# Regrouping the products of exponentials and v in an attention stage into two pairs

## The chip, the cores and the metric

The kernel runs on one core of a Trainium2 chip. Its engines work side by side, each through its own queue in order: TensorE (PE in the profile, its weight loads PEld), VectorE (DVE), ScalarE (ACT), GpSimd (POOL) and SyncE (SP), which issues most of the transfers. TensorE writes its results into PSUM banks, from which ACT and DVE take them. The metric is the device time of one execution in microseconds; the time of a version is the median of its runs.

## The reference

A transformer block over one sequence of 2048 tokens with 576 channels: adaptive layer norm, causal attention in four segments of 512 tokens with 32 heads of 18 channels and a memory of the earlier segments, then a second layer norm and a gated feed-forward network of 4608 channels. The change touches the attention inside a segment:

```python
for s in range(N):
    qs, ks, vs = q[:, :, s], k[:, :, s], v[:, :, s]
    logits = jnp.einsum("bhqd,bhkd->bhqk", qs, ks) * scale + mask
    p = _softmax(logits, axis=-1)
    a_dot = jnp.einsum("bhqk,bhkd->bhqd", p, vs)
    ...
    a_mem = num / den
    o = g * a_mem + (1.0 - g) * a_dot
```

## The kernel before

The kernel has three stages. The first projects q, k and v and writes them to DRAM. The second is the attention, with the output projection and the second layer norm woven into it. The third is the feed-forward network, which takes two thirds of the time and is bound by TensorE. Only the second stage is touched by the change.

The second stage goes over 32 units. Unit u = 8s + q is segment s and a group q of four heads. The order of all instructions is written out by hand (`manual_schedule`, L1160, and the loop at L1168): each turn of the loop has eleven steps, and each step emits three things.

- One step of `p2_step` (L565) for unit u: the logits, transposed, in a PSUM bank with tag s2 (two banks, L576), their exponential on ACT into the tile P0, P1, P2 or P3 (L579), and, at the end of each P, the causal mask on POOL (L583). Steps 0 to 3 fill P0 (keys 0 to 127, 512 queries), 4 to 7 fill P1 (384 queries), 8 and 9 P2 (256), 10 P3 (128).
- One step of `p1_step` (L164) for unit u + 2: the logits a second time, in a bank with tag s1 (two banks, L174), and the row maxima on DVE (L179). Its steps are equally wide, 512 for steps 0 to 3, 384 for 4 to 7, then 256 and 128. The maxima of a unit are transposed (`mt_a`, L193), copied and sent to DRAM (`mt_b`, L197 and L198) and loaded back (`load_m`, L161) as two more rows of q, so that the logits of `p2_step` come out with the maximum subtracted. A unit's first logits wait for that load.
- A list of events, from the table PAT (L54). It has four rows of eleven strings: row 0 for even units with q below 4, row 1 for odd ones, row 2 for even units with q of 4 and more, row 3 for odd ones. A step's events are emitted in the order of its string, behind the products of that step.

The events that matter here, as `event` (L807) resolves them:

- V0, V1 (of unit u) and V2, V3 (of unit u - 1): `av_step` (L587), the products of exponentials and v. Each is four products in fp32, one for each head, with 32 columns of the array each; they accumulate over V0 to V3 into one PSUM bank, av. V0 has 512 columns of queries, V1 384, V2 256, V3 128. A product in fp32 is two loads and two passes, so that a group shows as eight rows.
- E: the copy of av to SBUF on ACT (L608); c: four transposes of it (L617); d: division and weighting on DVE (L625 to L634).
- m and n: `mt_a` and `mt_b` with the load, for unit u + 1.
- M0 to M3 and X: a quarter each of the 14 products of a half row of the output projection (L694), and its addition on DVE (L699); R, S, T and Z, z prepare its operands by transposes (L666, L654) and copies.
- g and h: three activations on ACT (L743 to L745) and an addition on POOL for phi(q), in units with q below 5 and s below 3. D, G, A0, A1, B0, B1, C: the memory's part for q of 4 and more (products at L765, copies at L774).
- l, p, x: the second layer norm of a finished block, with an activation of 576 columns on ACT at x (L726), in odd units. Q, q, Y, P, f: small preparations.

The loop that emits them:

```python
            for k in range(11):
                next(ga, None)
                next(gb, None)
                for ev in PAT[q // 4 * 2 + u % 2][k].split():
                    event(ev, u)
```

Of the kernel before, what the change touches and what calls it, by code (L numbers as in the profile page):

```python
# [15 lines left out]
P = 128  # L16
S = 2048
D = 576
# [32 lines left out]
NE = 2  # L51
E1 = 3
E2 = 2
PAT = (["", "V2", "V3 E m D", "M0", "n M1 Q G", "c", "M2 d", "V0 g", "h A0 q M3 R S X", "T Y Z B0", "A1 P V1 z B1 f C"],  # L54
# [3 lines left out]
LNA = 1  # L58
S1B, S2B, XB, WB = 2, 2, 2, 1

# [6 lines left out]
def block(ctx: ExitStack, tc: tile.TileContext, x, wqk, wv, wo, beta, wgu, wd, c, w_mod, out):  # L67
# [1092 lines left out]
    with tc.manual_schedule():  # L1160
# [7 lines left out]
        for u in range(NU + 1):  # L1168
# [176 lines left out]
```

## Time and profile before

| | us |
|---|---|
| median of 3 runs | 1945.69 |
| lowest and highest run | 1944.17, 1946.47 |
| span of the profiled execution | 1946.8 |
| attention stage in it (first to last product of the 33 turns) | 260 to 618 |

The page gives no time of the profiled execution beside its span. In the rows of the timeline stand the start and the length in microseconds, the engine, the line, the operation, what it writes and reads, the size, and in brackets how long the engine was idle before it and what released it. A product's length includes its way through the array, so that successive products overlap; what one takes of TensorE's time is read from start to start. In the tables by stage, the columns are the stretch, its length, the busy time of PE, PEld, DVE, ACT and POOL with the number of instructions, the clock granted to TensorE (1 is full), the busy share of the DMA engines and the GB/s moved.

### The profile page before, as it was taken

How to read it: one execution, taken by the hardware profiler on the slowest of the kernel's cores; microseconds unless marked ns; L12 is line 12 of the kernel's file. 1: busy time of each engine (PE TensorE's matmuls, PEld its weight loads, DVE VectorE, ACT ScalarE, POOL GpSimd, SP SyncE). 2: the span in 40 equal slices, each digit the busy share in tenths (PEclk: the TensorE clock that was granted, in tenths of full speed). 3: DMA queues.
4: the chain of work that ended last, by engine and by line, in shares of the span. 5: the costliest groups of instructions: out<-in, count | busy, mean ns of one | idle time of the engine just before them, and what ended most of it. 6: DMA issues, size and time to landing. Idle time of an engine off the chain costs nothing.

```text
span 1946.8 us, 31901 instructions
## 1 busy us (share of the span) xinstructions
PE 1901.2 (98%) x11119; PEld 1593.1 (82%) x11119; DVE 1533.1 (79%) x3218; ACT 824.8 (42%) x1652; POOL 1020.6 (52%) x1396
## 2 busy tenths in 40 slices
PE   7999999999999899999999999999999999999999
PEld 4887865676766678888888888888888888888888
DVE  6575257878786999898898988979888888878886
ACT  2222256767667434344344343433333333333332
POOL 5322235455544866556565565556565564655551
PEclk9999999999999899999999999999999999999999
DMA  7776564444443332232222222174211211112111
GB/s 207 244 227 233 203 204 140 131 139 150 136 128 125 92 135 101 89 106 80 80 106 83 82 84 78 60 264 146 74 62 45 74 62 59 60 62 74 62 57 50
DMA packets 114354, 223.59 MB, mean 115 GB/s; under 512 B 22992, under 2 KB 40784, under 8 KB 112720
## 3 DMA queue, kind: packets, MB, share of 16 engines
q1 hardware_dynamic: 111936, 215.61, 34.2%
q0 software_dynamic: 576, 5.11, 0.7%
q8 instruction: 88, 1.44, 0.3%
q10 hardware_dynamic: 1680, 0.82, 0.2%
q14 instruction: 74, 0.61, 0.1%
HBM read 161.11 MB, written 60.36 MB: 114 GB/s over the span
## 4 chain that ended last, share of the span: by engine, by line
PE 88%; DVE 4%; DMA 4%; ACT 1%; issue 1%; POOL 1%; SPq 1%; POOLq 0%; ACTq 0%; DVEq 0%
PE M L1090 39%; PE pd L1152 23%; PE pp L93 4%; PE s L576 4%; PE av L596 4%; PE s L174 4%; PE pv L93 3%; PE pw L694 2%; DMA O<-in_wgu_dram 1%; DMA mD<-mr 1%; PE pn L765 1%; PE pm L429 1%; PE px L617 1%; PE pr L346 1%; DVE y L923 1%
## 5 line engine op out<-in xcount | busy, mean ns | idle before, releaser
L1090 PE MATMUL M<-y,wh 128*128 128x512 f32 x2520 | 792.0, 393 | 5.0 <-DVE cu L1106 2.1
L1090 PEld LDWEIGHTS M<-y,wh 128*128 128x128 f32 x2520 | 473.7, 188 | 101.7 <-issue 3.9
L1067 POOL TENSOR_TENSOR wh<-O,wh 32x128 fp32r<-32x128 f32 x504 | 296.6, 593 | 423.0 <-ACT wh L1065 271.3
L1090 PE MATMUL M<-y,wl 128*128 128x512 f32 x1008 | 394.7, 392 | 0.0
L1059 POOL TENSOR_TENSOR O<-O 128x384 f32<-128x384 f32 x288 | 315.4, 1095 | 75.0 <-DMA O<-in_wgu_dram 42.9
L1152 PE MATMUL pd<-dh,ah 128*128 128x288 f32 x1152 | 340.3, 295 | 0.2 <-DVE acc L1155 0.2
L1152 PE MATMUL pd<-dl,ah 128*128 128x288 f32 x1152 | 340.3, 295 | 0.0
L1152 PE MATMUL pd<-dh,al 128*128 128x288 f32 x1152 | 340.1, 295 | 0.0
L1110 ACT CAST ah<-sg 128x512 fp32r<-128x512 f32 x144 | 89.5, 621 | 547.8 <-DVE sg L1107 422.0
L1155 DVE TENSOR_TENSOR acc<-acc,pd 128x576 f32<-128x576 f32 x288 | 216.5, 752 | 111.8 <-PE pd L1152 108.4
L1066 DVE TENSOR_TENSOR wl<-O,wh 128x256 fp32r<-128x256 f32 x504 | 286.2, 568 | 6.0 <-ACT wh L1065 5.2
L179 DVE CUSTOM_DVE_ANT_0 junk<-s,tri 128x256 bf16<-128x256 f32 (+3 forms) x512 | 228.7, 487 | 77.2 <-PE s L174 69.8
L1065 ACT CAST wh<-O 128x384 fp32r<-128x384 f32 x504 | 242.8, 507 | 0.0
L1152 PEld LDWEIGHTS pd<-dl,ah 128*128 128x128 f32 x1152 | 217.4, 189 | 11.8
L1152 PEld LDWEIGHTS pd<-dh,ah 128*128 128x128 f32 x1152 | 216.7, 188 | 11.6 <-DVE acc L1155 0.6
L579 ACT ACTIVATE Pt<-s 128x512 f32<-128x512 f32 (+1 forms) x352 | 186.5, 559 | 88.1 <-PE s L576 72.0
L1152 PEld LDWEIGHTS pd<-dh,al 128*128 128x128 f32 x1152 | 216.6, 188 | 0.0
L1090 PEld LDWEIGHTS M<-y,wl 128*128 128x128 f32 x1008 | 190.0, 188 | 29.6
L1102 ACT ACTIVATE sg<-sg 128x512 f32<-128x512 f32 x144 | 91.2, 633 | 222.7 <-DVE sg L1101 222.7
L576 PE MATMUL s<-qs,ks 110*128 110x512 f32 (+2 forms) x384 | 150.5, 409 | 5.7 <-DMA qs<-mD 4.4
L174 PE MATMUL s<-ks,qs 108*128 108x256 f32 (+3 forms) x512 | 141.2, 327 | 3.3 <-DMA ks<-kD 1.4
L583 POOL TENSOR_SCALAR_AFFINE_SELECT Pt<-Pt 128x512 f32<-128x512 f32 x128 | 81.6, 648 | 100.6 <-ACT Pt L579 100.2
(428 smaller groups left out, 2836.6 us busy)
## 6 DMA issues: line engine op xcount, KB each, us to landing
O<-in_wgu_dram SPq DMA_DIRECT2D x72, 768.0 KB
ks<-kD SPq DMA_DIRECT2D x68, 216.0 KB
qs<-qD SPq DMA_DIRECT2D x68, 216.0 KB
kD<-fh SPq DMA_DIRECT2D x16, 512.0 KB
qD<-fh SPq DMA_DIRECT2D x16, 512.0 KB
yD<-st SPq DMA_DIRECT2D x28, 256.0 KB
y<-yD SPq DMA_DIRECT2D x7, 1024.0 KB
wml<-in_w_mod_dram SPq DMA_DIRECT2D x24, 216.0 KB
```

The source lines that it names most:

```text
L93: nc.tensor.matmul(ps, lhsT=a, rhs=b, start=(k == 0), stop=(k == 13))
L174: nc.tensor.matmul(bank[:, n * (h - h0):n * (h - h0) + n], lhsT=qst[b][0:108, h, 128 * i:128 * i + 128], rhs=kst[b][0:108, h // 2, 0:n], s ...
L179: nc.vector.tensor_tensor_reduce(junk[:, :n], bank[:, n * (h - h0):n * (h - h0) + n], tri[:, L - n:], 1.0, -3e38, op0=ALU.add, op1=ALU.max ...
L576: nc.tensor.matmul(bank[:, n * (g - h):n * (g - h + w)].rearrange("p (a b) -> p a b", a=w), lhsT=kst[u % NB][0:110, g // 2, 128 * j:128 * ...
L579: nc.scalar.activation(pt[:, h:h + per, :n], bank[:, :n * per].rearrange("p (a b) -> p a b", a=per), AF.Exp, scale=SCALE)
L1059: nc.gpsimd.tensor_tensor(o[:, d], o[:, a], o[:, b], op=op)
L1065: nc.scalar.copy(wh, o)
L1066: later.append(lambda: nc.vector.tensor_tensor(wl, o[:, 0:2], f32(wh[:, 0:2]), op=ALU.subtract))
L1067: later.append(lambda: nc.gpsimd.tensor_tensor(wh[32:64, 2], o[32:64, 2], f32(wh[32:64, 2]), op=ALU.subtract))
L1090: nc.tensor.matmul(bank, lhsT=a, rhs=b, start=(n == 0), stop=(n == 6))
L1152: nc.tensor.matmul(pd[:, h, :288], lhsT=a[:, tk], rhs=w[:, f, sl], start=(k == 0), stop=(k == 5))
L1155: nc.vector.tensor_tensor(o, o, pd[:, :, :288], op=ALU.add)
```

## The change

V0 moves from step 6, 7 or 8 to step 10, directly ahead of V1. V2 and V3, which stood in different steps (0 to 2 and 2 or 3), both come in step 2, V2 directly ahead of V3. The transpose of the maxima, m, stands behind V3 in all rows; in row 3 it stood behind V2 in step 1. In row 0 and row 2, A1 and the other events of step 10 stand behind V1. In row 3, l, D, p and G stay in step 2, M0 of that step goes behind the pair, n moves from step 2 to step 3 and E from step 4 to step 2. No other event changes its step, and nothing else in the kernel changes.

```diff
-PAT = (["", "V2", "V3 E m D", "M0", "n M1 Q G", "c", "M2 d", "V0 g", "h A0 q M3 R S X", "T Y Z B0", "A1 P V1 z B1 f C"],
-       ["V2 D", "l M0 Q", "V3 m E", "M1", "G p n A0 B0 M2", "", "M3 X A1 q c x d B1", "f", "V0 g", "", "C V1 Y h P"],
-       ["", "V2", "V3 m E", "M0", "D G M1 c n", "", "Q V0 d g R", "h", "M2 q M3 A0 S B0 X", "Z Y", "P f z V1 A1 T B1 C"],
-       ["", "V2 m", "l D n p G M0", "V3", "M1 E M2 A0", "", "M3 x c", "B0", "V0 d Q", "A1 g", "q X V1 Y B1 h P C f"])
+PAT = (["", "", "V2 V3 m E D", "M0", "n M1 Q G", "c", "M2 d", "g", "h A0 q M3 R S X", "T Y Z B0", "V0 V1 A1 P z B1 f C"],
+       ["D", "l M0 Q", "V2 V3 m E", "M1", "G p n A0 B0 M2", "", "M3 X A1 q c x d B1", "f", "g", "", "V0 V1 C Y h P"],
+       ["", "", "V2 V3 m E", "M0", "D G M1 c n", "", "Q d g R", "h", "M2 q M3 A0 S B0 X", "Z Y", "V0 V1 A1 P f z T B1 C"],
+       ["", "", "V2 V3 m E l D p G M0", "n", "M1 M2 A0", "", "M3 x c", "B0", "d Q", "A1 g", "V0 V1 q X Y B1 h P C f"])
```

## The prediction

> **What bounds the kernel now.** I read the page's head first, then the table by stage for the attention part (33 turns of the loop over units, 260 to 618 us, the only place the change touches), then the timeline of single units, last its waits.
>
> ```profile
> span 1946.8 us, 31901 instructions
> PE 1901.2 (98%) x11119; PEld 1593.1 (82%) x11119; DVE 1533.1 (79%) x3218; ACT 824.8 (42%) x1652; POOL 1020.6 (52%) x1396
> 260.38:349.40 89.02, 80.90 (x541) 48.90 (x540) 68.01 (x284) 63.57 (x131) 47.51 (x83) 0.96 0.49 146
> 349.40:578.71 229.31, 229.09 (x1703) 160.09 (x1699) 185.99 (x780) 163.71 (x328) 117.74 (x244) 1.00 0.46 138
> 578.71:618.40 39.69, 39.31 (x311) 25.68 (x307) 22.86 (x94) 27.42 (x55) 16.75 (x34) 1.00 0.25 81
> 474.78:485.68 10.90, 10.90 (x84) 7.35 (x80) 9.77 (x48) 8.70 (x17) 4.39 (x10) 1.00 0.61 172
> ```
>
> The columns of the table are length, then busy time of PE, weight loads, DVE, ACT, POOL, then clock. From unit 8 on (349 us) PE is busy without a gap, 229.09 of 229.31 us; in the first eight units it has 8 us of gaps. But DVE (81%) and ACT (71%) are not far behind: in unit 19, an odd one, DVE works 9.77 of 10.90 us. So TensorE time saved here shows in the span only while the two engines that empty its PSUM banks keep up, step by step, since they have two banks each (S1B, S2B). I write s(k) for the logits product of step k (L576, emptied by the exponential on ACT), s1(k) for the one of the maximum pass (L174, emptied by DVE), V0 to V3 for the groups.
>
> **The saving of a pair.** Steps 0 to 3 of unit 10:
>
> ```profile
> 370.52 0.50 PE L576 MATMUL s<-qs,ks 110*128 110x512 f32 x1
> 370.86 0.40 PE L174 MATMUL s<-ks,qs 108*128 108x512 f32 x1
> 371.10 0.40 PE L576 MATMUL s<-qs,ks 110*128 110x512 f32 x1
> 371.12 1.08 ACT L579 ACTIVATE Pt<-s 128x512 f32<-128x512 f32 x2 [0.34 <-PE s L576]
> 371.33 0.40 PE L174 MATMUL s<-ks,qs 108*128 108x512 f32 x1
> 371.39 0.69 DVE L179 CUSTOM_DVE_ANT_0 junk<-s,tri 128x512 bf16<-128x512 f32 x1 [0.56 <-POOL Pt L583]
> 371.67 0.64 PE L596 MATMUL av<-Pt,vq 128*32 128x256 f32 x8
> 372.24 0.50 PE L576 MATMUL s<-qs,ks 110*128 110x512 f32 x1
> 372.90 0.43 PE L596 MATMUL av<-Pt,vq 128*32 128x128 f32 x8
> 373.26 0.29 PE L193 MATMUL pmt<-ident,mc 128*32 128x128 f32 x1
> 373.30 0.48 PE L576 MATMUL s<-qs,ks 110*128 110x512 f32 x1
> ```
>
> A 512-wide product takes its place for 0.23-0.24 us (370.86 to 371.10, 371.10 to 371.33). Before V2 it is 0.34 (371.33 to 371.67), so entering costs 0.10. The first s behind any group takes 0.34 too (370.52 to 370.86), so leaving costs another 0.10. Inside, V2 (256 wide) takes 0.57 and V3 (128) 0.36: 0.21 for each 128 columns leaves 0.14-0.15 fixed. The Trainium skill, page TensorEngine Tiling (Array Packing), section Tiling Modes, says that changing the tiling mode drains the engine; these groups use 32 columns, their neighbours 128, and the two 0.10 agree with it. By that rule alone, with the drains as the only price, a pair would save 0.20 and the sum would be that of rival 2 below.
>
> A pair saves one entry and one exit, 0.20, for certain. Whether the second group's weights load under the first's products, sparing 0.12 of the fixed part, is not shown cleanly. One back-to-back V2 and V3 stands in the trace, of unit 31, where no other work is left:
>
> ```profile
> 616.96 1.22 POOL L583 TENSOR_SCALAR_AFFINE_SELECT Pt<-Pt 128x512 f32<-128x512 f32 x2 [0.17 <-ACT Pt L579]
> 617.64 0.16 PEld L596 LDWEIGHTS av<-Pt,vq 128*32 128x32 f32 x8 [1.07 <-POOL Pt L583]
> 618.23 0.16 PEld L596 LDWEIGHTS av<-Pt,vq 128*32 128x32 f32 x8 [0.43 <-POOL Pt L583]
> ```
>
> V3 follows V2 after 0.59, no better than alone, but it waited for its mask (616.96+1.22 = 618.18). In each group all eight loads start within the first moments, ahead of the second half of the products, so I take 0.31 a pair, and keep 0.19 as the other end. Order by engine: nothing is added or removed; V0 goes behind step 10 in all units, V2 and V3 meet in step 2. For 32 units and two pairs: 64 x 0.31 = 20 us of TensorE, if nothing waits. What follows a V does not come late: av is evacuated in step 2 as before, in the second odd pattern two steps sooner; each P buffer is rewritten only behind its V in PE's order; SP's order is the same.
>
> **What V2 covered (step 1).** With V2 gone from step 1, s(2) follows s1(1) directly. s(2) needs the bank of exp(0): 371.12+0.58 (one such exponential, row at 379.16 below) and 0.05 for the signal (618.18 to 618.23 above), 371.75 against 371.56 without the wait. s1(2) then needs the bank of DVE(0): 371.39+0.69+0.05 = 372.13 against 371.99. V2 starts at 372.13+0.34 = 372.47; V2, V3 and the transpose take 0.57+0.36+0.04-0.12 = 0.85; the next s stands at 373.32. Before: 373.30. The first pair gives nothing: 0.31 saved, 0.33 waited (0.19 for ACT, 0.14 for DVE). This holds wherever three steps now run bare: even units of both kinds, and the second odd pattern, where M0 moves behind the pair. In the first odd pattern M0 stays in step 1 and fills the gap; there DVE (9.77 of 10.90 us) is what is late, so I take 0 (ends -0.3, +0.3). So 32 first pairs: 0.
>
> **What V0 covered (steps 6 to 8).** Unit 10, steps 7 to 10:
>
> ```profile
> 376.86 0.34 PE L174 MATMUL s<-ks,qs 108*128 108x384 f32 x1
> 377.06 0.49 ACT L579 ACTIVATE Pt<-s 128x384 f32<-128x384 f32 x1 [0.26 <-PE s L576]
> 377.13 1.07 PE L596 MATMUL av<-Pt,vq 128*32 128x512 f32 x8
> 377.45 0.62 ACT L743 ACTIVATE qe<-qf 128x512 f32<-128x512 f32 x1
> 378.13 0.50 PE L576 MATMUL s<-qs,ks 110*128 110x512 f32 x1
> 378.46 0.40 PE L174 MATMUL s<-ks,qs 108*128 108x256 f32 x2
> 379.16 0.58 ACT L579 ACTIVATE Pt<-s 128x512 f32<-128x512 f32 x1
> 379.58 0.48 PE L576 MATMUL s<-qs,ks 110*128 110x512 f32 x1
> 380.15 0.41 PE L576 MATMUL s<-qs,ks 110*128 110x256 f32 x2
> 380.39 0.56 PE L174 MATMUL s<-ks,qs 108*128 108x128 f32 x4
> 380.88 0.85 PE L596 MATMUL av<-Pt,vq 128*32 128x384 f32 x8
> 381.66 0.50 PE L576 MATMUL s<-qs,ks 110*128 110x512 f32 x1
> ```
>
> From 377.45 ACT runs three phi activations, so exp(8) is at 379.16 whatever PE does, and frees its bank at 379.74. Without V0 (1.00, and 0.20 of entry and exit) s(10) is reached at 378.95 and waits until 379.79; before it stood at 380.15. Then 0.73 to the group (380.15 to 380.88), V0 and V1 back to back 1.00+0.78-0.12 = 1.66, and the next unit starts at 382.18: +0.52. The same walk gives +0.5 in unit 18, +0.8 in unit 8 (no output products yet) and +0.4 in unit 16 (four more transposes in between); units 0 and 1 +0.7 and +0.5; behind unit 2 the next one waits for its loads anyway. Estimates all, from these durations. Even units without phi, or with M2, M3 and A0 between, hide ACT: -0.3 or -0.2 each, nine of them, -2.4. Units 30 and 31, without a maximum pass: 0.
>
> Second odd pattern (units 13, 15, 21, 23), steps 8 and 9 of unit 21:
>
> ```profile
> 505.98 0.40 PE L174 MATMUL s<-ks,qs 108*128 108x256 f32 x2
> 506.25 0.47 ACT L579 ACTIVATE Pt<-s 128x384 f32<-128x384 f32 x1
> 506.30 1.07 PE L596 MATMUL av<-Pt,vq 128*32 128x512 f32 x8
> 507.30 0.50 PE L576 MATMUL s<-qs,ks 110*128 110x512 f32 x1
> ```
>
> ACT's normalisation (L726, 0.87 us) stands ahead of exp(7), whose bank comes free at 506.25+0.47+0.05 = 506.77; s(9) would be ready at 505.98+0.24 = 506.22. So 0.55 of waiting against 0.31: +0.24 each, +1.0. In this pattern the transpose m and the copy n also move back by a step (0.47), the two waits (0.33) and V3 (0.36), 1.2 us, and with them the load of the maxima; the next unit waits for that where DMA is slow:
>
> ```profile
> 328.88 0.47 PE L576 MATMUL s<-qs,ks 110*128 110x512 f32 x1 [0.95 <-DMA qs<-mD]
> ```
>
> Unit 6 waited 0.95 us for it already, so all 1.2 us show once. **Sum:** 0 - 2.4 + 2.3 (units 8, 10, 16, 18) + 1.2 (units 0, 1) + 1.0 + 1.2 = +3.3 us. One more window at half clock I add at +1: 1.7 us of bare waiting arise in unit 0, and the trace has such a window in unit 4:
>
> ```profile
> 302.50:307.10 4.60, 2.09 (x17) 0.97 (x20) 2.40 (x12) 1.75 (x5) 3.59 (x6) 1.00 0.37 126
> 307.10:310.50 3.40, 3.40 (x21) 1.48 (x14) 1.49 (x6) 1.59 (x4) 0.00 (x0) 0.50 0.77 215
> ```
>
> after a stretch where PE worked 2.09 of 4.60 us. The profiled span, 1946.8, lies 1.1 above the median of the runs, 1945.69, so I add +4.3 to the median: **1950.0 us**. With 0.19 a pair, some 40 pairs that stand on PE lose 0.12 each more: 1954.8.
>
> **The rivals.** (1) Faster: the waits are absorbed, because ACT and DVE finish all their banks during the 1.66 us of V0 and V1 and begin the next unit ahead. PE has no gap in units 9 to 29, so 21 x 2 x 0.31 = 13 us come through: 1932.7; half of it, 1939. For it speaks the full PE row; against it that a lead of two banks is used up in two steps, while the waits computed stand at the third and the eleventh. It decides once the wait per unit is under 0.6 us. (2) No prefetch between the groups of a pair: 1954.8, slower; the only back-to-back row does not exclude it. (3) More half-clock windows: 3.40 us at half clock do the work of 1.7, so each costs up to 1.7; three more give 1955; only the starting units have long enough gaps. (4) The terms cancel, 1946; my per-unit numbers are differences of a few tenths, and 0.1 in 32 units is 3 us. That the groups are not back to back after all I exclude: the order on PE shows them so.
> The Trainium skill, page TensorEngine Tiling (Array Packing), section Performance Considerations, warns that tiling speeds up TensorE but not PSUM evacuation; by that rule the bare steps run at the pace of DVE (0.69 us for a 512-wide pass) and not of PE (0.47 for both products), which is the mechanism of my forecast.
>
> **How the numbers follow.** Forecast (own range 1947 to 1954) 0.45, rival 1 0.20, rival 2 0.17, rival 3 0.06, rival 4 0.12. A measurement can tell about 0.2% (3.9 us) from no change, so "slower" begins at 1949.6. Of the forecast some two fifths (0.18) lie below that. Slower 0.27+0.17+0.06 = 0.50, same 0.18+0.12 = 0.30, faster 0.20. The range, 1937 to 1957, leaves out the larger half of rival 1 and the ends of 2 and 3.
>
> **What would show it.** Right: V0 to V1 start to start near 0.87 instead of 1.00, V2 to V3 0.45; new idle of PE before s(2) (ACT), s1(2) (DVE) and, in units 8, 10, 16, 18, about 0.8 us before s(10) for ACT. Wrong: no such idle and units of 10.3 to 11.7 us from 9 to 29 (rival 1); 1.00 and 0.57 in the pairs (rival 2); more than one added window with clock 0.5 (rival 3).

## The result and the profile after

| | median | lowest, highest | ratio, 95% interval |
|---|---|---|---|
| before (6 runs beside it) | 1946.08 us | 1941.54, 1947.35 | |
| after (6 runs) | 1951.57 us | 1949.89, 1955.18 | 1.0035 [1.0024, 1.0046] |

The change costs 5.5 us by the medians; the interval, times 1946.08, is 4.7 to 9.0 us, so the loss is clear of the noise, though small. The ratio is estimated from all runs and is not the quotient of the two medians (1.0028). The forecast was 4.3, with 1937 to 1957 as the range. The spans of the two profiled executions, 1946.8 and 1948.2, differ by 1.4 only, but the ends outside the touched stage hide most of it: the first logits stand at 255.8 instead of 260.3 us, and what follows the stage is 1.0 shorter. From the first product of the logits to the last of the groups the stage takes 365.0 us (255.8 to 620.8) after 358.1 (260.3 to 618.4): 6.9 longer.

The table by stage of the kernel after, cut at units 0, 8 and 28, and unit 19 by itself; the columns are those of the prediction's first fence:

```profile
255.80:347.77 91.97, 82.63 (x541) 50.67 (x539) 68.15 (x285) 63.78 (x131) 47.74 (x84) 0.96 0.48 142
347.77:579.77 232.00, 227.81 (x1702) 166.86 (x1698) 183.62 (x777) 162.38 (x328) 117.74 (x245) 1.00 0.47 137
579.77:620.74 40.97, 39.49 (x307) 27.04 (x307) 22.34 (x90) 28.04 (x55) 15.95 (x32) 1.00 0.24 74
475.91:486.90 10.99, 10.80 (x83) 7.75 (x79) 9.14 (x40) 8.53 (x17) 4.05 (x9) 1.00 0.60 164
```

All three stretches are longer: by 2.95, 2.69 and 1.28 us. In the middle one PE had no gap (229.09 of 229.31); now it is idle for 4.2 us. The busy column fell by 1.3 only: a product's modelled length reaches past the next one's place, so waits of a tenth or two do not show as idle and are read from start to start. Who is waited for, in two fences of the table of waits (total us, times, longest), first before, then after, each over the whole stage. The first row counts idle time of PE; the second is of weight loads, which show such short waits where PE's busy column doesn't:

```profile
PE s L576 <- ACT Pt L579: 1.1, 5, 0.5
PEld s L174 <- DVE mx L179: 3.4, 14, 0.5
```

```profile
PE s L576 <- ACT Pt L579: 7.5, 18, 1.4
PEld s L174 <- DVE mx L179: 11.8, 44, 0.9
```

ACT and DVE, which empty the two pairs of banks, are what PE now waits for more often; its idle waits for loads fell from 7.0 to 3.0 us, all in units 0 to 7. The weight loads of L576 that stand behind ACT fell as well, from 37.2 to 30.6 us, so that the sums alone settle little and the steps have to be walked. Unit 10, in which the prediction walked through the steps, shows both places. Steps 0 to 3 after:

```profile
370.10 0.50 PE L576 MATMUL s<-qs,ks 110*128 110x512 f32 x1
370.43 0.40 PE L174 MATMUL s<-ks,qs 108*128 108x512 f32 x1
370.67 0.40 PE L576 MATMUL s<-qs,ks 110*128 110x512 f32 x1
370.91 0.40 PE L174 MATMUL s<-ks,qs 108*128 108x512 f32 x1
371.34 0.49 PE L576 MATMUL s<-qs,ks 110*128 110x512 f32 x1
371.73 0.49 PE L174 MATMUL s<-ks,qs 108*128 108x512 f32 x1
372.15 0.86 PE L596 MATMUL av<-Pt,vq 128*32 128x256 f32 x16
372.94 0.28 PE L193 MATMUL pmt<-ident,mc 128*32 128x128 f32 x1
372.98 0.48 PE L576 MATMUL s<-qs,ks 110*128 110x512 f32 x1
```

V2 and V3 are one row of sixteen now. s(2) stands 0.43 behind s1(1) where a bare product takes 0.24: 0.19 of waiting for ACT. s1(2) stands 0.39 behind s(2): 0.15 for DVE. And V2 stands 0.42 behind s1(2), where 0.34 was the rule before: a cost that the prediction did not have. The weight loads show where it comes from, the bare s1(1) of before first (its product starts at 371.33), then s1(2) of after (371.73):

```profile
371.10 0.19 PEld L174 LDWEIGHTS s<-ks,qs 108*128 108x128 f32 x1
```

```profile
371.72 0.19 PEld L174 LDWEIGHTS s<-ks,qs 108*128 108x128 f32 x1 [0.20 <-DVE mx L179]
```

A bare product's weights are loaded 0.23 us ahead of it, under the product before. Where the product has to wait for its bank, its load waits too and starts together with it. That holds for s(2) as well, so that 0.1 of s1(2)'s 0.15 would be there without DVE. Steps 9 and 10:

```profile
378.43 0.41 PE L174 MATMUL s<-ks,qs 108*128 108x256 f32 x2
379.49 0.50 PE L576 MATMUL s<-qs,ks 110*128 110x256 f32 x2 [0.64 <-ACT Pt L579]
379.83 0.56 PE L174 MATMUL s<-ks,qs 108*128 108x128 f32 x4
380.31 1.71 PE L596 MATMUL av<-Pt,vq 128*32 128x512 f32 x16
381.96 0.50 PE L576 MATMUL s<-qs,ks 110*128 110x512 f32 x1
```

s(10) stands 0.82 behind the place it could have (378.43 + 0.24), and the row names the exponential. V0, V1 and their exit take 1.65.

### The profile page after: what moved, and what is told of

Its sections match the earlier page's. It is cut to its first block, busy times and chain, and to the rows that moved or that the text cites. A ratio compares the mean times of both kernels' runs of the same rounds, so it can differ in the third digit from the quotient of the medians.

```text
span 1948.2 us, 31881 instructions
## 1 busy us (share of the span) xinstructions
PE 1896.9 (97%) x11119; PEld 1599.4 (82%) x11119; DVE 1528.7 (78%) x3218; ACT 824.2 (42%) x1652; POOL 1018.6 (52%) x1396
## 4 chain that ended last, share of the span: by engine, by line
PE 85%; DVE 5%; DMA 4%; ACT 2%; issue 1%; POOL 1%; SPq 0%; ACTq 0%; POOLq 0%; DVEq 0%
PE M L1090 39%; PE pd L1152 23%; PE pp L93 4%; PE av L596 4%; PE s L576 4%; PE s L174 3%; PE pv L93 3%; PE pw L694 2%; DMA O<-in_wgu_dram 1%; ACT Pt L579 1%; DMA mD<-mr 1%; DVE junk L179 1%; PE pn L765 1%; PE pm L429 1%; DMA wm<-in_w_mod_dram 0%
## 5 line engine op out<-in xcount | busy, mean ns | idle before, releaser
L576 PE MATMUL s<-qs,ks 110*128 110x512 f32 (+2 forms) x384 | 149.3, 406 | 10.9 <-ACT Pt L579 7.5
L174 PE MATMUL s<-ks,qs 108*128 108x256 f32 (+3 forms) x512 | 145.3, 336 | 4.5 <-DVE mx L179 2.1
L583 POOL TENSOR_SCALAR_AFFINE_SELECT Pt<-Pt 128x512 f32<-128x512 f32 x128 | 81.6, 649 | 102.9 <-ACT Pt L579 102.1
```

The source lines that it names most:

```text
L174: nc.tensor.matmul(bank[:, n * (h - h0):n * (h - h0) + n], lhsT=qst[b][0:108, h, 128 * i:128 * i + 128], rhs=kst[b][0:108, h // 2, 0:n], s ...
L576: nc.tensor.matmul(bank[:, n * (g - h):n * (g - h + w)].rearrange("p (a b) -> p a b", a=w), lhsT=kst[u % NB][0:110, g // 2, 128 * j:128 * ...
```

## The experiments

All differences between the kernels are read unit by unit: from a unit's first logits to the next unit's, in the trace of one execution each, less the same in the trace before. A wait at a unit's first logits so counts in the unit ahead of it. The lines of the diffs below are cut from the rows of PAT, at one end or both. In the table, "rows" are the rows of PAT in units 8 to 29 (row 0: units 8, 10, 16, 18, 24, 26; row 1: the units after these; row 2: 12, 14, 20, 22, 28; row 3: the units after these).

| kernel | median, before beside it | ratio, 95% interval | stage | units 0-7 | row 0 | row 1 | row 2 | row 3 | 30, 31 |
|---|---|---|---|---|---|---|---|---|---|
| after | 1951.57, 1946.08 | 1.0035 [1.0024, 1.0046] | +6.9 | +3.0 | +2.9 | +0.6 | -0.7 | +0.1 | +1.0 |
| e1 first pair only | 1946.38, 1944.34 | 1.0015 [1.0005, 1.0026] | +5.4 | +4.3 | +0.4 | -1.1 | +0.5 | +0.5 | +0.9 |
| e2 second pair only | 1951.66, 1944.34 | 1.0045 [1.0029, 1.0062] | +6.6 | +0.1 | +2.5 | +3.5 | -1.1 | +1.4 | +0.1 |
| e3 M0 as filler | 1945.50, 1944.34 | 1.0011 [1.0000, 1.0021] | +1.3 | +1.4 | +0.9 | +0.7 | -2.6 | -0.2 | +1.1 |
| e4 phi late | 1948.54, 1944.34 | 1.0024 [1.0010, 1.0038] | +2.3 | -1.2 | +0.2 | +2.9 | -0.7 | +0.1 | +1.0 |
| e5 combined | 1954.40, 1943.62 | 1.0044 [1.0029, 1.0059] | +9.3 | +1.8 | +2.8 | -0.6 | +2.7 | -1.7 | +4.3 |
| e6 norm late | 1967.03, 1943.62 | 1.0112 [1.0092, 1.0132] | +20.0 | +1.0 | +9.5 | +0.7 | +4.5 | 0.0 | +4.3 |
| e7 rows mixed | 1940.51, 1944.09 | 0.9985 [0.9976, 0.9993] | -6.2 | -1.1 | -2.0 | -1.6 | -2.5 | -0.2 | +1.1 |
| e8 rows by unit | 1937.70, 1944.09 | 0.9969 [0.9958, 0.9980] | -6.3 | -0.8 | -2.0 | -0.8 | -2.6 | -0.2 | +0.1 |
| e9 norm late, nb early | 1951.53, 1944.09 | 1.0036 [1.0018, 1.0053] | +9.4 | +5.7 | +2.9 | +0.7 | -0.7 | 0.0 | +0.9 |
| e10 rows, nb early | 1938.25, 1943.87 | 0.9975 [0.9963, 0.9986] | -8.7 | -0.7 | -2.0 | -2.1 | -2.5 | -1.8 | +0.3 |

How well a cell is known is seen in e9, whose rows are those of after but for the place of two instructions (x and the nb that feeds it): in units 8 to 29 the two agree to 0.05 in every unit, most to 0.02, but in units 0 to 7, which wait for loads and fall into half-clock windows, their sums are +3.0 and +5.7. Only the right half of the table is read to tenths, and there too a late load can fall into a cell: unit 11 has the same row in e7, e8 and e10, but took -0.07, +0.62 and -0.52 us against before, because the first logits of unit 12 waited 0.44, 1.10 and 0 us for the load of the maxima. That is most of the difference of these three in the column of row 1.

**e1 and e2: which pair costs.** Each is the changed kernel with one of the pairs taken apart again. Row 0 of e1 and of e2, the other rows alike; in e1 the moves of m, n, E and M0 come with the first pair:

```diff
 e1
-"M2 d", "g", "h A0 q M3 R S X", "T Y Z B0", "V0 V1 A1 P z B1 f C"]
+"M2 d", "V0 g", "h A0 q M3 R S X", "T Y Z B0", "A1 P V1 z B1 f C"]
...
 e2
-["", "", "V2 V3 m E D", "M0",
+["", "V2", "V3 E m D", "M0",
...
```

> Only V2 and V3 are paired in step 2 (with m, n, E, M0 as in the changed kernel); V0 stays in steps 6 to 8 and V1 in step 10. My theory: the pair saves about 0.34 us a unit and the three bare steps ahead of it give it back (s(2) waits for ACT, s1(2) for DVE), so the attention stage keeps its length of before within -1 to +3 us, total 1945 to 1949. Rival, all of the loss comes from V0: the stage is 8 to 11 us shorter, total about 1936.

> Only V0 is moved behind step 10, next to V1; V2, V3, m, n and E stay as before. My theory: V0 no longer covers ACT's phi activations and the layer norm activation, so units 0, 1, 8, 10, 16, 18 get 0.4 to 1.0 us longer and the even units of q 4 to 7 get 0.2 to 0.3 shorter; the stage gets 1 to 5 us longer than before, total 1947 to 1951. Rival, V0 covered nothing that matters and the loss is the first pair's: 8 to 11 us shorter, total about 1936.

The first pair gives +0.3 over the 22 units from 8 on (0.4 - 1.1 + 0.5 + 0.5): nothing, as forecast, but as a balance: +0.1 a unit in rows 0, 2 and 3, and -0.2 in row 1, where M0 stays as filler. The whole stage is 5.4 longer, over the -1 to +3 expected, 4.3 of it in units 0 to 7 (the time, 1946.38, is where it was expected). The second pair costs 6.3 in the 22 units, and the stage is 6.6 longer for the 1 to 5 expected, the time 0.7 over its range: the odd units, which the expectation did not have, lose most. Both together cost 3.0, less than the sum of the parts, so that the two interact, in the odd rows (row 1: +3.5 for the second pair alone, +0.6 for both; row 3: +1.4 and +0.1). One odd unit of e2 shows what is late. Unit 19, steps 9 and 10:

```profile
483.83 0.50 PE L576 MATMUL s<-qs,ks 110*128 110x512 f32 x1
484.60 0.50 PE L174 MATMUL s<-ks,qs 108*128 108x256 f32 x2 [0.26 <-DVE mx L179]
484.94 0.40 PE L576 MATMUL s<-qs,ks 110*128 110x256 f32 x2
```

In row 1 it is DVE: s1(9) stands 0.77 behind s(9), which bare is 0.24, and 0.26 of it the row gives as idle. In the kernel before, V0 directly ahead of s(9) covered that, and s1(9) came 0.33 behind s(9). In row 3 it is ACT. Unit 21 of e2, from s1(8) to s(9):

```profile
507.60 0.40 PE L174 MATMUL s<-ks,qs 108*128 108x256 f32 x2
508.41 0.50 PE L576 MATMUL s<-qs,ks 110*128 110x512 f32 x1 [0.41 <-ACT Pt L579]
```

0.81 where a bare product takes 0.24: a wait of 0.57, the 0.55 that the prediction's walk had for the norm. Units 13, 15, 21 and 23 of e2 are 0.29 to 0.34 longer than before.

**e3: M0 as filler of the first pair.** M0 (three products of the output projection) goes to step 1, where V2 had been, in rows 0, 2 and 3.

```diff
-["", "", "V2 V3 m E D", "M0",
+["", "M0", "V2 V3 m E D", "",
...
-["", "", "V2 V3 m E l D p G M0", "n",
+["", "M0", "V2 V3 m E l D p G", "n",
```

> The changed kernel with M0 (three or four output products) taken from step 2 or 3 to step 1 in pattern rows 0, 2 and 3, where the steps ahead of the pair ran bare. My theory: TensorE then has 0.4 us of work in the gap and s(2), s1(2) come when their banks are free; 18 units with output products gain 0.2 to 0.4 us each, 4 to 7 us off the changed kernel, total about 1946. Rival, the waits there are not the cause (they only move): within 1 us of the changed kernel.

The even units from 10 to 28, which have output products, are 0.3 to 0.4 shorter than after, and the ratio falls from 1.0035 to 1.0011, with intervals that just do not meet. Row 3 gains next to nothing (-0.2 for +0.1): with its entry filled, s(9) waits for ACT as in e2 (0.75 behind s1(8) in unit 21, 0.34 in after). Unit 20, first after, then e3:

```profile
487.73 0.40 PE L174 MATMUL s<-ks,qs 108*128 108x512 f32 x1
488.11 0.50 PE L576 MATMUL s<-qs,ks 110*128 110x512 f32 x1
488.54 0.50 PE L174 MATMUL s<-ks,qs 108*128 108x512 f32 x1
488.97 0.86 PE L596 MATMUL av<-Pt,vq 128*32 128x256 f32 x16
```

```profile
488.34 0.30 PE L694 MATMUL pw<-woh,oh 128*128 128x288 f32 x1
488.48 0.29 PE L694 MATMUL pw<-wol,oh 128*128 128x288 f32 x1
488.61 0.30 PE L694 MATMUL pw<-woh,ol 128*128 128x288 f32 x1
488.75 0.40 PE L576 MATMUL s<-qs,ks 110*128 110x512 f32 x1
488.99 0.44 PE L174 MATMUL s<-ks,qs 108*128 108x512 f32 x1
489.36 0.86 PE L596 MATMUL av<-Pt,vq 128*32 128x256 f32 x16
```

With 0.41 us of other products in step 1, s(2) and s1(2) go at their bare pace (0.24) and V2 follows s1(2) after 0.37, not 0.43. In unit 20 that leaves 0.56 of gain over before, with two pairs at some 0.3 each: what was promised comes out where the bare steps are filled.

**e4: the three phi activations behind V0 and V1.**

```diff
-"M2 d", "g", "h A0 q M3 R S X", "T Y Z B0", "V0 V1 A1 P z B1 f C"],
+"M2 d", "", "A0 q M3 R S X", "T Y Z B0", "V0 V1 g h A1 P z B1 f C"],
...
-"M3 X A1 q c x d B1", "f", "g", "", "V0 V1 C Y h P"],
+"M3 X A1 q c x d B1", "f", "", "", "V0 V1 g C Y h P"],
```

> The changed kernel with phi's three activations (g) and its addition (h) moved from steps 7 and 8 to step 10, behind V0 and V1, in pattern rows 0 and 1, so that ACT does them while TensorE works on the pair. My theory: the wait of s(10) for ACT goes away in units 0, 1, 8, 10, 16, 18, 3 to 6 us off the changed kernel, total 1946 to 1949. Rival, phi only moves the wait to the first logits of the next unit: within 1 us of the changed kernel.

Against after, units 8, 10, 16 and 18 are shorter by 0.66, 0.89, 0.24 and 0.89: the wait of s(10) was for the exponential behind phi on ACT. Units 9 and 17 lose 1.1 each, the ones behind the units with q = 0, in which the copy of z (L660 on ACT) now follows phi: DVE waits 1.57 us for that copy (its subtraction at L661 starts at 356.90), and in unit 9 s1(2) then 0.46 us for DVE. So the rival was half right, and units 8 to 29 gain only 0.5 us over after in sum; the two intervals overlap. In e5 z goes ahead of phi, and units 9 and 17 are free of it (0.00 and -0.45).

**e5: all of it, and a late norm.** M0 as in e3; g and h late with z ahead of them; in row 1 only the first pair; and in row 3 the norm's activation (x, L726) moved from step 6 to step 10, since the prediction charged it 0.24 a unit.

```diff
-PAT = (["", "", "V2 V3 m E D", "M0", "n M1 Q G", "c", "M2 d", "g", "h A0 q M3 R S X", "T Y Z B0", "V0 V1 A1 P z B1 f C"],
-       ["D", "l M0 Q", "V2 V3 m E", "M1", "G p n A0 B0 M2", "", "M3 X A1 q c x d B1", "f", "g", "", "V0 V1 C Y h P"],
-       ["", "", "V2 V3 m E", "M0", "D G M1 c n", "", "Q d g R", "h", "M2 q M3 A0 S B0 X", "Z Y", "V0 V1 A1 P f z T B1 C"],
-       ["", "", "V2 V3 m E l D p G M0", "n", "M1 M2 A0", "", "M3 x c", "B0", "d Q", "A1 g", "V0 V1 q X Y B1 h P C f"])
+PAT = (["", "M0", "V2 V3 m E D", "", "n M1 Q G", "c", "M2 d", "", "A0 q M3 R Z S X", "T Y z B0", "V0 V1 g h A1 P B1 f C"],
+       ["D", "l M0 Q", "V2 V3 m E", "M1", "G p n A0 B0 M2", "", "M3 X A1 q c x d B1", "f", "V0 g", "", "C V1 Y h P"],
+       ["", "M0", "V2 V3 m E", "", "D G M1 c n", "", "Q d g R", "h", "M2 q M3 A0 S B0 X", "Z Y", "V0 V1 A1 P f z T B1 C"],
+       ["", "M0", "V2 V3 m E l D p G", "n", "M1 M2 A0", "", "M3 c", "B0", "d Q", "A1 g", "V0 V1 x q X Y B1 h P C f"])
```

> Each row keeps what paid there. Rows 0, 2 and 3 have both pairs, with M0 in step 1; row 0 has phi (g, h) behind V0 and V1 and the copies of the output operand (Z, z) two steps earlier, so that ACT is free for phi; row 3 has the layer norm activation (x) behind V0 and V1; row 1 has the first pair alone, with V0 and phi in step 8 as before. My theory: where TensorE is full (units 8 to 29) row 0 gains 0.5, row 1 0.2, row 2 0.55, row 3 0.3 us a unit over the kernel before; the attention stage is 6 to 10 us shorter than before, total about 1937. Rival, the gains don't add because a wait removed comes back in the next unit: within 2 us of before.

**e6: the late norm alone**, on the changed kernel.

```diff
-"M3 x c", "B0", "d Q", "A1 g", "V0 V1 q X Y B1 h P C f"])
+"M3 c", "B0", "d Q", "A1 g", "V0 V1 x q X Y B1 h P C f"])
```

> The changed kernel with only the activation of the layer norm (x) moved in row 3 from step 6 to step 10, behind V0 and V1. My theory: exp(7) is no longer late, the 0.55 us that s(9) waits for ACT goes away, and units 13, 15, 21 and 23 get 0.3 to 0.5 us shorter than in the changed kernel, in all 1 to 2 us. Rival, these units are held by DVE or by the pair at the end: under 0.1 us each.

Both missed, and by the same step: e6 alone loses 15 us to after. The loss is not in row 3, where x stands, but in the units behind it (against before: unit 14 +3.1, 16 +3.8, 22 +1.6, 24 +3.6, 30 +4.0). Unit 14 of e6, POOL, then ACT, then PE:

```profile
416.03 0.81 POOL L634 TENSOR_TENSOR o<-o,tmp 128x288 f32<-128x288 f32 x1 [1.19 <-DVE tmp L633]
416.79 1.23 POOL L583 TENSOR_SCALAR_AFFINE_SELECT Pt<-Pt 128x512 f32<-128x512 f32 x2
...
418.77 0.27 POOL L725 TENSOR_SCALAR nb<-mv,rs 128x1 f32<-128x1 f32 x1
...
419.07 0.87 ACT L726 ACTIVATE xh<-xr,nb,rs 128x576 f32<-128x576 f32 x1 [2.74 <-POOL nb L725]
419.84 0.39 ACT L774 COPY nm<-pn 128x304 f32<-128x304 f32 x1
420.14 1.08 ACT L579 ACTIVATE Pt<-s 128x512 f32<-128x512 f32 x2
...
420.79 0.79 PE L576 MATMUL s<-qs,ks 110*128 110x512 f32 x1 [1.92 <-ACT Pt L579]
```

The activation needs nb, one number for each row, from POOL. At x's old place this costs next to nothing (in after, ACT is idle for 0.1 us before the eleven activations together); at the new one nb stands behind an addition, which itself waits 1.19 us for DVE, two masks and the rounding of the maxima. ACT waits 2.74 us for it with two exponentials queued behind, and PE 1.92 for them. Then the clock takes its share:

```profile
417.30:420.70 3.40, 1.56 (x12) 0.68 (x4) 1.85 (x7) 1.63 (x4) 1.91 (x7) 1.00 0.00 0
420.70:424.10 3.40, 3.31 (x21) 1.73 (x22) 0.70 (x2) 1.71 (x4) 0.43 (x2) 0.51 0.69 206
```

After a window in which PE worked 1.56 of 3.40 us, the next 3.40 us run at a granted clock of 0.51, which costs 1.7. The clock's records have such a window of 3.41 us in units 14, 16, 24 and 30, the four that lose 3.1 us and more; unit 22, +1.6, has none. The wait of 1.9 and the clock's 1.7 make the 3.3 us by which this unit is longer than after's (15.42 to 12.11), some 0.3 being made up later.

**e7, e8 and e9: the cause put to the test.** e7 is e5 with x back in step 6. e8 takes e7's rows in units 8 to 29 and those of before elsewhere. e9 is e6 with nb computed in step 2, right behind what it needs; the activation stays late, and the two lines are taken out of its place.

```diff
 e7
-"M3 c", "B0", "d Q", "A1 g", "V0 V1 x q X Y B1 h P C f"])
+"M3 x c", "B0", "d Q", "A1 g", "V0 V1 q X Y B1 h P C f"])
 e8
-                for ev in PAT[q // 4 * 2 + u % 2][k].split():
+                for ev in (PAT if 8 <= u < 30 else PAB)[q // 4 * 2 + u % 2][k].split():
 e9
         nc.gpsimd.tensor_tensor(rs, rs, mhalf[:, :1], op=ALU.pow)
+        nbs[0] = nb = o3.tile([P, 1], F32, tag="nb", name="nb")
+        nc.gpsimd.tensor_scalar(nb, mv[:, 0:1], rs[:, 0:1], -1.0, op0=ALU.mult, op1=ALU.mult)
```

> Rows 0 to 2 as in the combined schedule (e5), row 3 as in the schedule with M0 in the entry (e3), so that the layer norm's Identity is back in step 6. Theory: the loss of e5 came from that Identity alone; its units 14, 16, 22, 24 and 30 go back to the lengths of the kernel before or less. Taken unit by unit from e5 and the changed kernel: units 0 to 7 +1.8, row 0 of units 8 to 29 -2.2, row 1 -2.1, row 2 -2.3, row 3 about +0.1, units 30 and 31 +1.0, together -3.7 us: 1940 against 1943.6. Rival: the moves in rows 0 to 2 have a cost of their own in the units after them; then units 14, 16, 22, 24 stay 1.2 us or more above before and the time is 1948 to 1954.

> The rows of e7 in units 8 to 29 only, the rows of before in units 0 to 7, 30 and 31. Theory: what the pairs cost is in units that end on a load or a flush (0 to 7, 30, 31), not in the groups; then only the gains are left, -6.5 us for units 8 to 29: 1937 against 1943.6, ratio 0.9967. Rival: the units in which the time is lost are set by chance from run to run; then e8 stands with e7, 1940 to 1943.

> e6 with one instruction taken out of the way: the bias nb (POOL, 0.27 us) is computed in step 2, right behind the power that it needs, not in step 10; the Identity stays in step 10. Theory: in e6 the Identity waited for nb behind POOL's selects and additions (15.3 us in 6 waits), and every exponential behind it on ACT with it; then the waits for nb are gone and the time is that of the changed kernel, 1949 to 1954. Rival: the late Identity blocks SP's queue through its store of xh, ahead of the loads of the next unit; then 1963 to 1968 stays.

The times of all three came out as expected. e9 takes 1951.5 us, and ACT never waits for nb, where e6 had 15.3 us of that in 6 waits: POOL's queue was the cause of e6, not the store on SP. e7 and e8 are faster than before, e8 by 6.4 us (1937.70 to 1944.09). That the old rows help in units 0 to 7 is not shown: e8's sum there is -0.8, e7's -1.1, both within the scatter named above. In units 30 and 31, +1.1 against +0.1 is the rows' doing. The two profiled stages are equally long (-6.2 and -6.3), with 1.1 us of a late load in e8's unit 11, and the two intervals still overlap a little. The table by stage of e8, units 8 to 27:

```profile
347.89:572.07 224.18, 220.78 (x1703) 166.39 (x1699) 183.07 (x779) 161.49 (x328) 118.03 (x244) 1.00 0.48 142
```

PE's busy time is 8.3 us less than before in this stretch (229.09 to 220.78), and 3.4 of idle time stay.

**e10: what the norm costs in its old place.**

```diff
 e8 to e10: nb as in e9, and in row 3
-"M3 x c", "B0", "d Q", "A1 g", "V0 V1 q X Y B1 h P C f"])
+"M3 c", "B0", "d Q", "A1 g", "V0 V1 x q X Y B1 h P C f"])
```

> e8 with the layer norm's Identity of row 3 in step 10 and its bias nb in step 2 (both as in e9). It asks whether the Identity (0.87 us on ACT) in step 6 costs a row-3 unit anything, as the prediction's +0.24 said. In e9 against the changed kernel its move gave nothing (0.00 to -0.1 per unit), but in e5, where M0 fills the entry of the first pair, the four odd units of that kind were 0.35 us shorter than in e7, which differs from it in those units by the Identity alone. Theory: the Identity is hidden as long as another wait ends later (that of the entry), and shows when that one is filled: row 3 of units 8 to 29 goes from -0.2 to about -2 us, and the time is 2 us under e8, 1935 to 1936 beside e8's 1937.7. Rival: e5's odd units were short because of the long ones ahead of them, which left ACT and POOL ahead; then e10 stands with e8, ratio 0.997.

Row 3 goes from -0.2 to -1.8 us, as the theory said. Unit 21 around s(9), first e8, then e10 (the lines are four further down than in the kernel before: L580 is the logits, L583 the exponential, L178 the maximum's product):

```profile
501.12 0.40 PE L178 MATMUL s<-ks,qs 108*128 108x256 f32 x2
501.88 0.50 PE L580 MATMUL s<-qs,ks 110*128 110x512 f32 x1 [0.35 <-ACT Pt L583]
```

```profile
499.62 0.40 PE L178 MATMUL s<-ks,qs 108*128 108x256 f32 x2
499.96 0.50 PE L580 MATMUL s<-qs,ks 110*128 110x512 f32 x1
```

0.76 from start to start in e8, 0.34 in e10. The time does not show it: 0.9975 [0.9963, 0.9986] beside e8's 0.9969 [0.9958, 0.9980], and 1938.25 us for the 1935 to 1936 expected. An effect of 1.6 us is under what these intervals can tell (half a width is 2.1 us), so whether e10 is the better kernel stays open; both beat the kernel before.

## Why the prediction came out as it did

The sign and the place were right, and the size nearly so (+5.5, forecast +4.3), this in part by luck. Against the terms of the sum, the stage took more in units 0 and 1 (1.4), in the other even units (2.7), the phi units (0.5), row 1 (0.6), unit 29 (0.3) and units 30 and 31 (1.0), and less for the norm (1.2), the load of the maxima (1.7) and the clock window (1.0). Errors of 6.5 and 3.9 us leave the 2.6 by which the stage (+6.9) is over the forecast. Step by step:

- **The saving of a pair** was right. From the records of the single products, V0 to V1 takes 0.882 (forecast 0.87) where V0 to its successor took 0.997, and V2 to V3 0.456 (0.45) where it was 0.570, medians of 32. So the second group's weights do load under the first's products (in unit 10 V3's loads begin at 372.39, its products at 372.61), and rival 2 falls. The Trainium skill, page TensorE: Matmul & The Clock Gate, section Step-by-step: what each phase is for, says that loads may be pulled ahead of products in flight, while products keep their order; these 0.11 agree.
- **The first pair gives nothing:** right by mechanism, with waits of 0.19 and 0.15 (forecast 0.19 and 0.14). In sum too (e1: +0.3 over 22 units), but there row 1's -1.1, for which the forecast had 0, hides +1.4 in the others. The walk had 2.80 us from the first s to the one behind the pair; it is 2.88. The missing 0.1 is V2's place, 0.42 behind s1(2) and not 0.34, because s1(2) waited and its own weights load late. In the records the median is 0.425 (0.330 before); wherever the load of s1(2) starts together with its product, V2 follows after 0.42 to 0.44, and where it starts 0.2 ahead, as in nearly all units before, after 0.32 to 0.33. In units 8 to 29 of after, thirteen have the full 0.1, and the excess sums to 1.5 us, as much as the gap between the forecast's +1.4 for these units (1.8 for row 0, -1.3 for row 2, 1.0 for row 3) and the +3.0 measured. That was a term left out, though not the only difference: row 0 took 2.9, row 1 0.6, row 2 -0.7, row 3 0.1.
- **V0 moved, phi units:** right by mechanism, 0.5 us too low in sum. Units 8, 10, 16, 18 took +0.89, +0.72, +0.45, +0.73 (forecast +0.8, +0.5, +0.4, +0.5). In unit 10 s(10) comes 9.39 us after the first s (forecast 9.27), the pair and its exit take 1.65 (1.66). e4 shows ACT's phi as the cause.
- **V0 moved, row 1:** the prediction had no term for it. Alone it costs +3.5 us in six units (e2: s1(9) waits for DVE, which has 9.77 of 10.90 us of work there); with the first pair, which gains 1.1 there, the row takes +0.6. That the missing term stayed small was luck.
- **The gain in nine other even units** was mis-sized: eight of them (4, 12, 14, 20, 22, 24, 26, 28) give -0.7 where -0.27 each make -2.1. e3 shows the rest of it behind the bare steps: filled, row 2 alone gives -2.6.
- **The norm ahead of exp(7) in row 3, +0.24 each,** failed: 0.0 measured. The wait that the walk computed for s(9), 0.55, is there with the second pair alone (e2: 0.57, and +0.31 a unit) and in e8 (0.76 less 0.24, 0.52), but not in after, whose unit 21 has

```profile
507.26 0.40 PE L174 MATMUL s<-ks,qs 108*128 108x256 f32 x2
507.60 0.51 PE L576 MATMUL s<-qs,ks 110*128 110x512 f32 x1
```

  with 0.34, a wait of 0.10. In after PE reaches s(9) later, because the three bare steps of the first pair have already held it up. Two waits behind one another were added where the first covers the second; filling the first (e3, e8) or leaving it out (e2) uncovers the other, and e10 removes it.
- **The load of the maxima, +1.2 once at unit 6:** failed. The wait for the load at the start of unit 6 is shorter than before, 0.27 us for 0.95, and unit 5, which ends with it, is 0.5 shorter. In the other runs this wait is anything from 0 to 0.94, so that one execution says little of the term. Unit 6 itself is 0.9 longer, but that is something else:

```profile
326.06 0.47 PE L576 MATMUL s<-qs,ks 110*128 110x512 f32 x1 [0.27 <-DMA qs<-mD]
...
333.95 0.50 PE L174 MATMUL s<-ks,qs 108*128 108x256 f32 x2 [0.28 <-DVE mx L179]
```

  It is longer from inside, where s1(9) waits for DVE, V0 being gone from step 6. e2, in which m and n are not moved, has +0.7 in the same unit.
- **A half-clock window more:** in its place, not in number. The window of unit 0 is twice as long, 6.8 us, and the one of unit 4 is gone, so that the two profiles have the same amount in this stage:

```profile
265.00:272.00 7.00, 6.67 (x27) 3.35 (x28) 1.63 (x10) 2.24 (x5) 4.37 (x7) 0.51 0.59 182
```

  Units 0 and 1 took +2.6 (forecast +1.2), but e9 with the same rows there has +3.9 and half-clock windows of 13.7 us in units 0 to 7, while e2, e4 and e7 have none, so these units say little from one execution.
- **Units 30 and 31 at 0:** wrong, +0.6 and +0.4. e1 has it, e2 does not: it is the first pair. Without a maximum pass nothing but V2 stood between s(1) and s(2), and now PE waits for ACT there:

```profile
601.93 0.73 PE L576 MATMUL s<-qs,ks 110*128 110x512 f32 x2
603.11 0.50 PE L576 MATMUL s<-qs,ks 110*128 110x512 f32 x1 [0.45 <-ACT Pt L579]
```

- **Rival 1** (waits absorbed) was not what the change does, but its end can be reached: with M0 as filler, phi late and V0 split from V1 in row 1, units 8 to 29 give -5.6 us in e8 and, with the norm late and nb early, -8.3 in e10 (1.1 of this difference is the late load in e8's unit 11).
- **Rivals 3 and 4** fall: no half-clock window was added in the profiled execution, and the interval does not reach 1.

## What to carry to other kernels

Work that stands between products and saves nothing by being there may still be the cover under which other engines empty the banks; before grouping it, walk the bare steps against both evacuating engines, and put other ready work in the hole. Waits do not add: of two in one unit the first may hide the second, and the second then appears as soon as the first is removed, so that a fix is judged together with what it uncovers. An instruction that is moved takes its place in its engine's queue only with its inputs: move the small operation that feeds it early, on the other engine's queue, and read the loss in the units behind, not where the instruction stands.

## What the runs showed of the hardware

A product that waits for its PSUM bank also has its own weights loaded late: the load starts with the product (371.72 in unit 10) instead of 0.23 us ahead, and the next group follows after 0.42 instead of 0.34; 0.425 is the median of 29 units (0.330 before). The wait so costs some 0.1 us more than it lasts. The 0.34 of the first s behind a group looks the same in the records: its load starts with it, too (372.24 in unit 10 of before).

A wait of PE of 1.9 us in the middle of a fully busy stage was enough for a window at half clock (e6: 1.56 us of work in 3.40, then 3.40 us at 0.51), which nearly doubled its price; it happened four times in e6. Not every such wait has this price: in e4 one of 1.9 us ahead of unit 4 was followed by none. In e6 the windows start whole multiples of 3.41 us apart, so it may depend on where the wait falls; that is not shown. The Trainium skill, page TensorE: Matmul & The Clock Gate, section What's actually happening, gives windows of about 3.4 us and the lower clock after an idle one. The length agrees; that the window must be idle does not, since PE worked for nearly half of it here.
